# First group's key differences, queries and values loaded at other stages, last seeds stored after them, first maxima's rows put behind the first seeds

## The chip, the cores and the metric

The kernel runs on one core of a Trainium2 chip. The metric is the device time of one execution in microseconds; the time given is the median of several runs.

## The reference

Two independent halves are computed from float32 inputs and put side by side in the output, 2048 rows of 2 x 448.

```python
def _A_ref(u, log_A_real, A_imag, C_real, C_imag, log_dt, D_skip):     # D = 448, N = 256
    dt = jnp.exp(log_dt)
    A = -jnp.exp(log_A_real) + 1j * A_imag
    C = (C_real + 1j * C_imag) * dt[:, None]
    P = jnp.exp((A * dt[:, None])[:, :, None] * pos[None, None, :])
    K = 2.0 * jnp.einsum("dn,dnl->dl", C, P).real
    # y = causal convolution of u with K along the 2048 rows, by FFTs of length 4096
    return y + u * D_skip[None, None, :]

def _B_ref(x, wqkv, wo):                                               # 16 heads of 28
    q, k, v = (x @ wqkv) split into heads
    p = _softmax(einsum("bhqd,bhkd->bhqk", q, k) * Dh ** -0.5, axis=-1)
    return einsum("bhqk,bhkd->bhqd", p, v) merged @ wo
```

## The kernel before

The program has an opening, in which the projections of the attention and the "seeds" of the convolution kernel are computed and written to device memory, and a long second part that works through 16 units of attention, with the convolution's work put into slots between them.

**The opening.** It is a loop over 41 stages (`n_stage`). Each stage issues some of the 48 projection jobs (`work`): 4 chunks of 512 rows, in each 8 jobs for keys and queries (4 groups of heads, keys first: `qk_proj`) and 4 for values (`v_proj`; in the last chunk ahead of the keys). The jobs are spread evenly over the first 37 stages (`PW`). A job's matmuls go out in one call of `project`, its emptying from PSUM (`evac`) in the next: ScalarE writes a rounded high part into a tile `hl`, VectorE the remainder, and SyncE stores both to `k_d` or `q_d`. There are two `hl` tiles, so that a job's `evac` waits until the store of the job two before has landed. For the first two chunks `evac` also stores the key differences (`kd_d`).

Beside the projections run the seeds, in 8 parts (`seeds(o)`), four stages apart (`SP`); the 13 steps of a part go to successive stages (`slots`). The last two steps are its stores: `put_g` (tile `sg`, 11 stages after the part's start) and `put_e` (12 after). The tile that `put_e` stores is one of three tiles named `qhat`, the same three that hold the queries of a unit (`load_q`).

`ahead` says at which stage the first group's operands are loaded back: key differences (`load_kd`, 16 transfers, two a stage from stage `A0`), the first unit's queries (`load_q(0)`, two of its four transfers at stage `A1` and two at the next), keys of the heads 0 to 2 (`load_k(0, j)`, four transfers each, at the stages `KW`). The keys take the place of the projections' weights (`k0_t`), one head's place after another. In a stage, the seeds' steps and then `ahead` come behind the projections. At the last projection stage follow the fourth keys, the second unit's queries and the four tiles of values.

In this part no order is written by hand for the engines (`KEPT["p"]` is empty); a planner orders the instructions with the program's order as priority. All transfers are issued by SyncE.

After the loop come the row maxima of the first unit: 16 tiles, each with four matmuls (`max_mm`; the first reads the key differences, the other three the keys). The first matmul goes through ScalarE (`rl`), and VectorE reduces. `max_join` and `max_end` turn the maxima into two rows `mh`, and `max_put` stores those into two spare rows of the first unit's queries, so that the scores' matmul subtracts the maximum.

**The second part** keeps the program's order on every engine (`nc.kept = KEPT["a"]`). It begins with the loads of three parts of seeds (`load_sd`, tile `sdb`), the maxima of three tiles of the second unit (`LEAD`), the first use of the seeds, and the loads `u_load(0)` and `u_load(1)` (four transfers each, tile `ua`). Then come, for each of 256 steps, the scores (`s_mm`, tile `pss`), the exponentials, the product with the values (`po`), the maxima of the unit ahead, and a slot of the convolution.

All instructions are recorded under one helper line (L75), so that rows of the profile are told apart by their tiles.

Of the kernel before, what the change touches and what calls it, by code (L numbers as in the profile page):

```python
# [25 lines left out]
NQ = L // CQ  # L26
# [14 lines left out]
PS = 1  # L41
SGB, XB, XL = 2, 5, 4
K0, KP, KD, UP = 0, 3.5, 4, 3
A0, A1, KW = 26, 34, (33, 35, 36)

N1 = 32
N2 = 64
# [5 lines left out]
NO = 8  # L53
# [37 lines left out]
def body(ctx, tc, a, out):  # L91
# [53 lines left out]
    def load_k(g, j, p):  # L145
        if j == 0:
            t = k0_t if g == 0 else p.tile([128, HG, L], F32R, name="khat")
            kt_g[g] = [t[:, i] for i in range(HG)]
        for r in range(4):
            nc.sync.dma_start(kt_g[g][j][32 * r:32 * r + 32, :].bitcast(F32), k_d[g][r % 2, 32 * j:32 * j + 32, :])  # L150
# [3 lines left out]
    def load_v(g, c):  # L154
        v_g[g, c] = t = v_p.tile([128, NK // NQ, HG, 32], F32, name="v", bufs=5)
        nc.sync.dma_start(t.rearrange("p t h e -> p t (h e)"), v_d[c][:, g])
# [8 lines left out]
    def load_q(u, rows=range(4)):  # L165
        g, c = divmod(u, NQ)
        if 0 in rows:
            q_u[u] = q_p.tile([128, HG, CQ], F32R, name="qhat", bufs=3)
        t = q_u[u]
        for r in rows:  # L170
            nc.sync.dma_start(t[32 * r:32 * r + 32].bitcast(F32), q_d[g][c][r // 2].rearrange("(j p) q -> p j q", j=HG))
# [26 lines left out]
    def max_end(u, ps):  # L198
        nc.tensor.transpose(ps[:16, :128], m_u[u, 1], ident)
        mh = q_p.tile([16, 2, 128], F32R, name="mh")  # L200
        nc.vector.tensor_scalar(mh[:, 0, :], ps[:16, :128], -1.0, None, op0=ALU.mult)
        nc.vector.scalar_tensor_tensor(mh[:, 1, :], ps[:16, :128], -1.0, mh[:, 0, :].bitcast(F32),
                                       op0=ALU.mult, op1=ALU.subtract)
        mh_u[u] = mh

    def max_put(u):
        for i in range(2):
            nc.sync.dma_start(q_u[u][DH + i:DH + i + 1, :, :].rearrange("p h (t q) -> p (h t) q", t=4).bitcast(F32),
                                mh_u[u][:, i, :].bitcast(F32))


    with ExitStack() as st:
# [47 lines left out]
        t = a["A_log_dt"]  # L260
# [52 lines left out]
        def seeds(o):  # L313
# [87 lines left out]
            def factors(i, k, p_, n_):  # L401
                zz, mg = q["zz"], q["mg"]
                mul(vec, zz[:, i:i + 3, :, 0, :], vk(mg, k), vk(q["r"], k))
                mul(vec, zz[:, i:i + 3, :, p_, :], vk(mg, k), vk(q["sn"], k))
                for k in range(i, i + 3):
                    act.activation(zz[:, k, :, n_, :], zz[:, k, :, p_, :], AF.Copy, scale=-1.0)

            def cmul(e, dst, s0, n, wr, wi, conj):

                if e is nc.vector:  # L410
                    x_ = ps_x.tile([128, CQ], F32, name="px")[:, :BO * 16 * n].rearrange("p (b h e) -> p b h e", h=16, e=n)
                else:
                    x_ = s_p.tile([128, BO, 16, 4], F32, name="x_e")[:, :, :, :n]
                br, bi = (w_[:, :, :, None].to_broadcast([128, BO, 16, n]) for w_ in (wr, wi))
                for c in range(2):
                    mul(e, dst[c], s0[c], br)
                    mul(e, x_, s0[1 - c], bi)
                    e.tensor_tensor(dst[c], dst[c], x_, ALU.add if (c == 0) == conj else ALU.subtract)
# [3 lines left out]
            e3 = lambda: cmul(vec if o % 8 < E3 else pol, e8(3, 4), e8(1, 2), 1, q["e8"][:, :, 0, :, 2], q["e8"][:, :, 1, :, 2], False)  # L422
            e5 = lambda: cmul(pol, e8(5, 8), e8(1, 4), 3, q["e8"][:, :, 0, :, 4], q["e8"][:, :, 1, :, 4], False)
            put_e = lambda: nc.sync.dma_start(sd_d[o][:, :, :F_G].rearrange("b p f -> p b f"), q["se"])
            put_g = lambda: nc.sync.dma_start(sd_d[o][:, :, F_G:].rearrange("b p f -> p b f"), q["sg"])

            def load():
                if o not in nats:
# [2 lines left out]
            dts = lambda *r: [lambda i=i: times_dt(i) for i in r]  # L431
            fa, fb = lambda: factors(0, 3, 2, 1), lambda: factors(3, 8, 1, 2)
            return [[load], [exp_a] + dts(1, 2, 3), dts(0), [turn], [phases], [reduce], [sines], [sizes, g_base],
                    [places, fa, e_base], [e3, g_first], [fb, e5, g_copies], [put_g], [put_e]]

        xh, xl = {}, {}

# [58 lines left out]
        for c in range(NQ):  # L496
# [4 lines left out]
            if c + 1 < NQ:  # L501
                jobs[1] = (lambda c, f: lambda: (load_x(c + 1), f())[1])(c, jobs[1])
            work += jobs
        stages = [seeds(o) for o in range(NO)]
        n_stage = SP * (NO - 1) + len(stages[0])
        slots = [[] for _ in range(n_stage)]
        for o in range(NO):
# [5 lines left out]
        ahead = collections.defaultdict(list)  # L513
        for i in range(2 * HG):
            ahead[A0 + i].append(lambda i=i: load_kd(0, i // 2, range(2 * (i % 2), 2 * (i % 2) + 2)))
        for i in range(2):
            ahead[A1 + i].append(lambda i=i: load_q(0, range(2 * i, 2 * i + 2)))

        for j, t in enumerate(KW):
            ahead[t].append(lambda j=j: load_k(0, j, k0_p))  # L520

        def project():

            e = work.pop(0)() if work else None
            while pend:
                pend.pop(0)()
            if e:
                pend.append(e)

        for t in range(n_stage):  # L530
            while work and n_work - len(work) < n_work * (t + 1) / PW:
                project()
            for f in slots[t] + ahead.get(t, []):
                f()
            if t + 1 == PW:
                project()
                wst.close()
                load_k(0, HG - 1, k0_p)
                load_q(1)
                for c in range(NQ):  # L540
                    load_v(0, c)
        xst.close()
        more = [lambda: ps_t.tile([128, CQ], F32, name="pt")] * 2 + [w_tile] * 3
        for i in range(16):
# [2 lines left out]
        nc.scalar.activation(half_pi[:1], half_pi[:1], AF.Exp)  # L547
        max_join(0)
        max_end(0, ps_t.tile([128, CQ], F32, name="pt"))
        max_put(0)  # L550
        sst.close()


# [322 lines left out]
    def u_load(i):  # L876
        if i < 32:
            u_jobs[i][0]()
# [10 lines left out]

    u_load(0)  # L890
    u_load(1)
    u_due = collections.deque((3 + UP * i + (UP / 2) * c + (4 if i > 15 else 0), i, c) for i in range(32) for c in range(2))
    k_due = collections.deque(range(NB))
    m_due = collections.deque()
# [229 lines left out]
```

## Time and profile before

| | |
|---|---|
| median of 3 runs | 1322.6 us (1322.46 to 1323.23) |
| profiled execution | 1324.82 us |
| its span | 1323.0 us |
| mean granted TensorE clock | 0.973 |
| TensorE busy | 1235.2 us, 93% |
| VectorE, ScalarE, GpSimd busy | 75%, 72%, 63% |
| moved by DMA | 205.36 MB, 155 GB/s over the span |

The page and the trace are of one execution. PE is TensorE, PEld its weight loads, DVE VectorE, ACT ScalarE, POOL GpSimd, SPq the queue of SyncE, where an entry is the issue of a transfer and not the transfer itself. Times are microseconds from the start of the span. `khat` are keys (and, earlier, the projections' weights), `qhat` queries or a part's first seeds, `kdif` key differences, `sg` a part's other seeds, `mh` the maxima's rows, `rl` and `mx` the maxima's intermediate tiles.

### The profile page before, as it was taken

How to read it: one execution, taken by the hardware profiler on the slowest of the kernel's cores; microseconds unless marked ns; L12 is line 12 of the kernel's file. 1: busy time of each engine (PE TensorE's matmuls, PEld its weight loads, DVE VectorE, ACT ScalarE, POOL GpSimd, SP SyncE). 2: the span in 40 equal slices, each digit the busy share in tenths (PEclk: the TensorE clock that was granted, in tenths of full speed). 3: DMA queues.
4: the chain of work that ended last, by engine and by line, in shares of the span. 5: the costliest groups of instructions: out<-in, count | busy, mean ns of one | idle time of the engine just before them, and what ended most of it. 6: DMA issues, size and time to landing. Idle time of an engine off the chain costs nothing.

```text
span 1323.0 us, 33194 instructions
## 1 busy us (share of the span) xinstructions
PE 1235.2 (93%) x12625; PEld 705.6 (53%) x12625; DVE 989.7 (75%) x2138; ACT 953.3 (72%) x2068; POOL 839.9 (63%) x704
## 2 busy tenths in 40 slices
PE   6878886899999999999999999999998999898997
PEld 5657763455555555555555555555555545444433
DVE  5897786877778777778778988889887857757311
ACT  5876762488888888888888888888886656655553
POOL 3686682398887788887689999899992212211211
PEclk9979888899999999999999999999999999999999
DMA  6677669836765546478534134642325543824485
GB/s 204 204 263 257 218 210 286 230 69 139 183 146 133 128 137 172 130 182 215 165 99 93 55 85 94 149 96 56 97 56 146 189 154 132 276 91 165 148 221 137
DMA packets 200088, 205.36 MB, mean 155 GB/s; under 512 B 95992, under 2 KB 158520, under 8 KB 197880
## 3 DMA queue, kind: packets, MB, share of 16 engines
q1 hardware_dynamic: 199928, 203.23, 54.8%
q8 instruction: 100, 1.64, 0.5%
q14 instruction: 60, 0.49, 0.1%
HBM read 120.73 MB, written 82.18 MB: 153 GB/s over the span
## 4 chain that ended last, share of the span: by engine, by line
PE 69%; DVE 15%; POOL 5%; ACT 4%; issue 3%; DMA 2%; SPq 0%; ACTq 0%; POOLq 0%; DVEq 0%
PE pm L75 39%; PE po L75 15%; PE pss L75 15%; DVE mx L75 3%; DVE tri L75 2%; DVE p L75 2%; DVE pr L75 2%; DVE rl L75 1%; POOL e L75 1%; POOL qhat L75 1%; DVE qhat L75 1%; ACT tri L75 1%; DVE sg L75 1%; DVE px L75 1%; ACT p L75 1%
## 5 line engine op out<-in xcount | busy, mean ns | idle before, releaser
L75 ACT ACTIVATE p<-pss 128x512 f32<-128x512 f32 x1024 | 561.4, 610 | 120.8 <-PE pss L75 118.2
L75 PE MATMUL pss<-qhat,khat 128*128 128x512 f32 x1024 | 402.8, 399 | 2.3 <-ACT p L75 2.3
L75 DVE TENSOR_REDUCE mx<-pm 128x1 f32<-128x512 f32 x500 | 321.5, 684 | 101.8 <-PE pm L75 100.2
L75 PE MATMUL pm<-khat,qhat 128*128 128x512 f32 x749 | 327.1, 440 | 14.4 <-DVE mx L75 6.9
L75 POOL TENSOR_TENSOR e<-e,sdb 128x256 f32<-128x256 f32 x168 | 202.2, 1203 | 118.0 <-ACT e L75 108.8
L75 PE MATMUL po<-p,v 128*32 128x512 f32 x2048 | 270.1, 596 | 0.0
L75 POOL TENSOR_TENSOR e<-e,eu 128x256 f32<-128x256 f32 x168 | 248.4, 1479 | 13.2
L75 PEld LDWEIGHTS pm<-khat,qhat 128*128 128x128 f32 x749 | 141.6, 189 | 210.6 <-ACT p L75 43.6
L75 DVE CUSTOM_DVE_ANT_0 rl<-pm,rl 128x512 f32<-128x512 f32 x249 | 171.5, 689 | 59.9 <-ACT rl L75 56.0
L75 PEld LDWEIGHTS pss<-qhat,khat 128*128 128x128 f32 x1024 | 190.8, 189 | 47.8 <-issue 11.8
L75 POOL TENSOR_TENSOR eu<-e,sdb 128x256 f32<-128x256 f32 x168 | 202.3, 1204 | 0.0
L75 POOL TENSOR_TENSOR p<-pr,pr 64x448 f32<-64x448 f32 x32 | 40.9, 1279 | 197.5 <-DVE pr L75 186.5
L75 ACT ACTIVATE rl<-pm 128x512 f32<-128x512 f32 x249 | 150.9, 606 | 20.8 <-PE pm L75 20.7
L75 DVE TENSOR_TENSOR g<-g,zg 128x128 f32<-128x128 f32 x392 | 162.3, 414 | 3.4
L75 PE MATMUL pm<-xh,khat 112*128 112x512 f32 x256 | 92.9, 447 | 21.9 <-DVE hl L75 9.5
L75 PE MATMUL pm<-kdif,qhat 128*128 128x512 f32 x249 | 101.4, 407 | 2.4 <-DVE mx L75 1.3
L75 DVE TENSOR_TENSOR zg<-g,zg 128x128 f32<-128x128 f32 x224 | 88.0, 393 | 5.1
L75 PEld LDWEIGHTS pm<-e,g 128*32 128x32 f32 x3584 | 57.2, 109 | 43.7 <-issue 17.0
L75 PE MATMUL pm<-e,g 128*32 128x64 f32 x3584 | 73.1, 222 | 1.9 <-POOL e L75 1.9
L75 PEld LDWEIGHTS pm<-xh,khat 112*128 112x128 f32 x256 | 54.0, 216 | 37.8 <-DVE hl L75 10.9
L75 ACT ACTIVATE y<-pm 128x448 f32<-128x448 f32 x48 | 26.3, 549 | 66.1 <-issue 33.0
L75 PEld LDWEIGHTS po<-p,v 128*32 128x32 f32 x2048 | 55.8, 110 | 22.3 <-issue 17.9
(135 smaller groups left out, 1504.6 us busy)
## 6 DMA issues: line engine op xcount, KB each, us to landing
sdb<-sd SPq DMA_DIRECT2D x56, 336.0 KB
khat<-k SPq DMA_DIRECT2D x64, 256.0 KB
qhat<-q SPq DMA_DIRECT2D x64, 256.0 KB
sd<-sg SPq DMA_DIRECT2D x8, 1456.0 KB
k<-hl SPq DMA_DIRECT2D x16, 512.0 KB
q<-hl SPq DMA_DIRECT2D x16, 512.0 KB
mw<-in_mw SPq DMA_DIRECT2D x16, 512.0 KB
sd<-qhat SPq DMA_DIRECT2D x8, 896.0 KB
```

The source lines that it names most:

```text
L75: i = f(*args, **kw)
```

## The change

The key differences are loaded from stage 16 on instead of 26. The first unit's queries are loaded at the stages 33 and 34 instead of 34 and 35. Three of the four value tiles are loaded at the stages 14, 23 and 31; the fourth stays after the fourth keys. In each stage, `ahead` now comes before the projections and the seeds' steps instead of behind them. The stores of the last two parts of the seeds leave their stages: they follow the loop, those of part 6 before the second unit's queries and those of part 7 behind them. `max_put(0)` moves from the end of the opening into the second part, behind the first seed loads, the three lead tiles and the two `u` loads.

```diff
-A0, A1, KW = 26, 34, (33, 35, 36)
+A0, A1, KW, V0 = 16, 33, (33, 35, 36), (14, 23, 31)
...
-                    [places, fa, e_base], [e3, g_first], [fb, e5, g_copies], [put_g], [put_e]]
+                    [places, fa, e_base], [e3, g_first], [fb, e5, g_copies], [put_g], [put_e]], [put_g, put_e]
...
         stages = [seeds(o) for o in range(NO)]
+        put_last = [f for o in range(NO - 2, NO) for f in stages[o][1]]
+        stages = [t if o < NO - 2 else t[:-2] + [[], []] for o, (t, _) in enumerate(stages)]
...
+        for c, t in enumerate(V0):
+            ahead[t].append(lambda c=c: load_v(0, c))
         for j, t in enumerate(KW):
             ahead[t].append(lambda j=j: load_k(0, j, k0_p))
...
         for t in range(n_stage):
+            for f in ahead.get(t, []):
+                f()
             while work and n_work - len(work) < n_work * (t + 1) / PW:
                 project()
-            for f in slots[t] + ahead.get(t, []):
+            for f in slots[t]:
                 f()
             if t + 1 == PW:
                 project()
                 wst.close()
                 load_k(0, HG - 1, k0_p)
-                load_q(1)
-                for c in range(NQ):
-                    load_v(0, c)
+                load_v(0, NQ - 1)
+        for f in put_last[:2]:
+            f()
+        load_q(1)
+        for f in put_last[2:]:
+            f()
...
         max_end(0, ps_t.tile([128, CQ], F32, name="pt"))
-        max_put(0)
         sst.close()
...
     u_load(0)
     u_load(1)
+    max_put(0)
```

## The prediction

> **What bounds the kernel now.** I read the page first: after an opening of some 250 us TensorE is busy nearly all the time, so whatever moves the end of the opening moves the end of the kernel by as much.
>
> ```profile
> span 1323.0 us, 33194 instructions
> ...
> PE 1235.2 (93%) x12625; PEld 705.6 (53%) x12625; DVE 989.7 (75%) x2138; ACT 953.3 (72%) x2068; POOL 839.9 (63%) x704
> ```
>
> Every edit lies in the opening. So I read the chain of waits next, from 190 us to the first scores. Its pieces are start, duration, what.
>
> ```profile
> 37.77 3.51 DMA k<-hl
> ...
> 203.56 11.49 DMA qhat<-q
> ...
> 255.44 0.43 PE pss L75
> ```
>
> The chain stands for 11.49 us in one load: the queries of the first unit. TensorE's timeline says the same from its side, and those of ScalarE and VectorE show what stands at the same place (start, duration, engine, operation, and in brackets the idle time before it and what ended it).
>
> ```profile
> 203.31 0.40 PE L75 MATMUL pm<-xl,khat 112*128 112x512 f32 x1
> 215.19 0.76 PE L75 MATMUL pt<-kdif,qhat 128*128 128x512 f32 x1 [11.48 <-DMA qhat<-q]
> ```
>
> ```profile
> 198.77 0.57 ACT L75 ACTIVATE hl<-pm 128x512 fp32r<-128x512 f32 x1
> 205.38 0.69 ACT L75 ACTIVATE hl<-pm,kones 128x512 fp32r<-128x512 f32 x1 [6.04 <-DMA k<-hl]
> ...
> 210.51 0.63 ACT L75 ACTIVATE hl<-pm 128x512 fp32r<-128x512 f32 x1
> ```
>
> ```profile
> 206.10 0.75 DVE L75 SCALAR_TENSOR_TENSOR hl<-pm,kones,hl 128x512 fp32r<-128x512 f32 x1 [3.49 <-ACT hl L75]
> ...
> 211.17 0.69 DVE L75 TENSOR_TENSOR hl<-pm,hl 128x512 fp32r<-128x512 f32 x1 [1.05 <-ACT hl L75]
> 216.62 0.69 DVE L75 CUSTOM_DVE_ANT_0 rl<-pt,rl 128x512 f32<-128x512 f32 x1 [4.76 <-ACT rl L75]
> ...
> 248.54 0.28 DVE L75 SCALAR_TENSOR_TENSOR mh<-pt,mh 16x128 fp32r<-16x128 f32 x1
> ```
>
> The projections end on TensorE at 203.71 (203.31 + 0.40), the first maximum begins at 215.19. But VectorE is done with the last projection only at 211.86 (211.17 + 0.69) and starts on the maxima at 216.62. From there to the finished maxima at 248.82 (248.54 + 0.28) it works through the first unit's tiles. So of TensorE's 11.48 us only VectorE's 4.76 can come back by an earlier load alone.
>
> Why the load is late stands in SyncE's queue, the only one that issues transfers, in program order:
>
> ```profile
> 180.25 0.47 SPq L75 DMA_DIRECT2D sd<-sg  x1
> ...
> 184.42 1.29 SPq L75 DMA_DIRECT2D sd<-qhat  x1
> ...
> 194.93 0.38 SPq L75 DMA_DIRECT2D q<-hl  x1
> ...
> 196.79 1.76 SPq L75 DMA_DIRECT2D khat<-k  x4
> ...
> 202.04 0.50 SPq L75 DMA_DIRECT2D sd<-sg  x1
> 202.59 1.78 SPq L75 DMA_DIRECT2D qhat<-q  x2
> ...
> 219.76 6.01 SPq L75 DMA_DIRECT2D khat<-k  x4
> ...
> 248.53 1.26 SPq L75 DMA_DIRECT2D qhat<-mh  x2
> 249.85 1.52 SPq L75 DMA_DIRECT2D sdb<-sd  x3
> 251.41 4.62 SPq L75 DMA_DIRECT2D ua<-in_A_u  x8
> ```
>
> The sizes of one transfer, from the page, and the traffic by stretch (length, engines' busy time, granted clock, share of the DMA engines, GB/s):
>
> ```profile
> sdb<-sd SPq DMA_DIRECT2D x56, 336.0 KB
> khat<-k SPq DMA_DIRECT2D x64, 256.0 KB
> qhat<-q SPq DMA_DIRECT2D x64, 256.0 KB
> sd<-sg SPq DMA_DIRECT2D x8, 1456.0 KB
> k<-hl SPq DMA_DIRECT2D x16, 512.0 KB
> ...
> sd<-qhat SPq DMA_DIRECT2D x8, 896.0 KB
> ...
> kdif<-kd SPq DMA_DIRECT2D x64, 64.0 KB
> v<-v SPq DMA_DIRECT2D x16, 256.0 KB
> ...
> ua<-in_A_u SPq DMA_DIRECT2D x64, 56.0 KB
> ```
>
> ```profile
> 80.00:110.00 30.00, 23.09 (x84) 18.62 (x84) 26.26 (x44) 23.75 (x49) 22.68 (x29) 0.80 0.52 181
> 180.00:192.00 12.00, 12.00 (x45) 9.48 (x43) 11.83 (x20) 6.05 (x8) 11.45 (x7) 0.82 1.03 358
> ...
> 196.00:248.00 52.00, 34.24 (x88) 18.77 (x86) 38.68 (x85) 15.11 (x31) 9.53 (x15) 0.82 1.03 286
> 228.00:236.00 8.00, 7.14 (x19) 3.09 (x18) 8.00 (x19) 2.61 (x5) 0.00 (x0) 1.00 1.05 244
> ```
>
> From 196 to 248 us the transfers run at their limit: four key loads take SyncE 6.01 us to issue at 219.76, 1.76 at 196.79. Order in the queue is order of landing there. I take stores at 358 GB/s (180 to 192 us is mostly stores) and loads at 244 (228 to 236 us is keys and queries): 512 KB stored 1.46 us, 1456 KB 4.16, 896 KB 2.56; a key load of 4 x 256 KB 4.30, half the queries 2.15. Before the first byte comes 2.05 us: the 3.51 of the unhurried store at 37.77 less 1.46. Tested on before, from 194.93: store of query rows 198.4, two key differences 199.0, keys 203.3, store 204.7, half the queries 206.9, store 208.3, seeds 212.5, other half 214.6. The trace has 205.38 for the fourth (ScalarE's wait) and 215.05 for the last (203.56 + 11.49): the walk is 0.4 to 0.7 us early, and I add 0.5.
>
> **The change, part by part.**
>
> *Key differences and values sooner.* Sixteen loads of 64 KB and three of 256 KB go to stages 14 to 31; nothing is added. The differences fall at about 80 to 125 us, where the DMA engines are 0.52 busy at 80 to 110; by 244 GB/s the sixteen take 4.3 us of 30. I take nothing for it. Its cover gone, it delays a projection's store, whose buffer ScalarE waits for: there is one such wait of 2.2 us at 60 to 90 us, so I bound it by 2.2 either way.
>
> ```profile
> ACT hl L75 <- DMA k<-hl: 2.2, 1, 2.2
> ```
>
> *First queries and keys sooner, last seeds later.* Half the queries and the first keys now stand behind the seeds of 184.42 and ahead of two projection stores; the other half behind the store of 194.93; the seeds of 202.04 behind the last keys. The walk, from 180.25: seeds 186.5, store 187.9, seeds 190.5, half the queries 192.6, keys 196.9, stores 198.4 and 199.9, other half 202.0, store 203.5, second keys 207.8, store 209.2. With 0.5 added the queries are there at 202.5, ahead of TensorE's 203.71, and leave the chain.
>
> *What is late next* is the emptying of the projections: VectorE at 211.86, ScalarE at 211.14 (210.51 + 0.63). Its own waits are for buffers, freed when earlier stores land. Against before, the store that ScalarE awaited at 205.38 lands 1.2 us sooner; the one freed for 198.77 comes at 200.4, 1.6 later; the one freed for 210.51 at 209.7, still in time. Bounds: VectorE's idle 3.49 us at 206.10 may go altogether, or the 1.6 and 0.9 (209.2 against 208.3) may both be lost, 2.5. Between them I take nothing, as the sooner and the later one meet in the same row. Gain: 4.76 us.
>
> The Trainium skill, "DMA: Bandwidth & Descriptors", section "Queues, rings and completion order", says that each DMA engine takes one issuing engine's descriptors in ring order. That speaks against putting 1.5 MB of loads ahead of the stores that ScalarE waits for. ScalarE's 6.04 us for a store agree. By this rule alone, with nothing landing sooner, the sum would be 4.76 - 2.5 = 2.3.
>
> *Second queries.* Their tile is one from which seeds are stored, so SyncE now waits at this load for a store just issued, and holds the last seeds and all below. The walk goes on: third keys 213.5, two stores 216.4, last keys 220.7, values 221.8, seeds 226.0 and 228.5, wait 2.05, queries 234.9. First use is after the maxima, 4.76 sooner than 248.82: 244.1. Nine us to spare: cost nothing.
>
> *Seeds and u ahead of the maxima's rows.* Those two small transfers now stand behind the last seeds (239.0, 241.6), three seed loads (1008 KB, 245.8) and eight of u (448 KB, 247.7): landed at about 248.7 with 0.5 added and 0.5 for themselves. SyncE issues the eleven while the maxima still run, before they cost 6.1 us after. The scores need the rows at 255.44 - 4.76 = 250.7, since the three lead tiles of the second unit stand ahead on TensorE. Two us to spare: cost nothing, gain nothing.
>
> Sum: 4.76 us. The profiled execution took 1324.82 us (span 1323.0), the median of the runs 1322.6. 1324.82 - 4.8 = 1320.0; the same off the median gives 1317.8. From 255 us on each engine keeps its order, so the shift reaches the end. The bound for a difference that can be told is 0.2%, 2.65 us.
>
> **The rivals.**
>
> *More comes back.* With the store of 205.38 sooner and no other later, VectorE's 3.49 us go too: 4.76 + 3.49 = 8.25, time 1314.3. For it: the walk has that store 1.2 sooner. Against: two others later.
>
> *The stores are late.* Both delays are lost (2.5) and a third wait of like size, 0.7, comes at the store landing at 198.9 for ScalarE's step just before 198.77: 4.76 - 3.2 = 1.6, time 1321.0, no difference to be told. For it: the order of the queue, and the rule above from "DMA: Bandwidth & Descriptors" of the Trainium skill. Against: the row of 6.04 gets shorter. That the change does not do what it says belongs here: no order is kept by hand in this phase, and a planner that left the loads where they were would give 1322.6. Before's queue follows the program text, so I hold that unlikely.
>
> *The maxima's rows become the wait*, and the kernel slower. From 199.9 to these rows SyncE now moves 13,072 KB, 13.39 MB. At the 286 GB/s of 196 to 248 us that is 46.8, with the 2.05 at the second queries 248.8. The gain is gone when the rows land at 255.44: 13.39 MB in 53.5 us, 250 GB/s. At the 225 GB/s of the stretch below it is 59.5 us, the rows come at 261.5, 6.0 late: 1328.6. For it: loads alone ran at 244. Against: the mix is before's, which made 286.
>
> ```profile
> 195.00:203.00 8.00, 8.00 (x22) 6.32 (x23) 5.20 (x12) 4.31 (x12) 5.45 (x11) 0.60 0.87 225
> ```
>
> **How the numbers follow.** Forecast 0.60, more comes back 0.15, stores late 0.15, maxima's rows 0.10. Faster by over 0.2%: 0.60 + 0.15 = 0.75; within 0.2%: 0.15; slower: 0.10. The likeliest gives 1317.8. The range goes down to 1314.3, the second case, and up to 1323.0, which holds the third and leaves the fourth out.
>
> **What would show it.** In the chain after, no load of the first queries; the first kdif matmul right after the projections or at VectorE's pace, its first reduction at 211 to 213; the stored maxima near 244; the first scores near 250.7, ended by a lead tile and not by a load. Late stores would show as longer idle times of ScalarE before hl than 6.04 us in all. If the first scores wait for the maxima's rows, the last part is wrong. If the opening shifts before 180 us, the first part is.

## The result: slower by 0.4%, because the opening was ordered anew

| | before | after |
|---|---|---|
| median | 1323.22 us (1322.46 to 1324.79) | 1328.43 us (1326.58 to 1330.24) |
| ratio, 95% interval | | 1.0039 [1.0026, 1.0053] |
| profiled execution | 1324.82 us | 1330.24 us |
| TensorE's last projection ends | 203.71 us | 216.12 us |
| first maximum starts on TensorE | 215.19 us | 215.91 us |
| maxima's rows ready on VectorE | 248.82 us | 254.86 us |
| first scores start | 255.24 us | 260.90 us |

The forecast was 1317.8 us, the range ended at 1323.0, and slower had a chance of 0.10.

The page of after answers to the first lines shown of before. TensorE has 5.1 us more to show as busy and the span is 5.5 us longer.

```profile
span 1328.5 us, 33194 instructions
...
PE 1240.3 (93%) x12625; PEld 708.9 (53%) x12625; DVE 986.7 (74%) x2138; ACT 955.4 (72%) x2070; POOL 836.3 (63%) x704
```

The chain of waits of after, at the place where before's had 11.49 us for the first queries (start, duration, what):

```profile
200.07 8.95 DMA k<-hl
...
209.10 0.70 ACT hl L75
...
209.82 0.76 DVE hl L75
...
210.63 5.49 PE pm L75 x12
216.12 0.83 PE pt L75 x2
```

No load of queries stands in it. A projection's store does: ScalarE can't empty the next projection before it has landed, and the last projection's matmuls follow. TensorE's timeline says the same: the first `kdif` matmul comes right behind the last projection, with no idle time named, and the scores follow lead tiles, not a load.

```profile
215.49 0.63 PE L75 MATMUL pm<-xl,khat 112*128 112x512 f32 x1
215.91 0.63 PE L75 MATMUL pt<-kdif,qhat 128*128 128x512 f32 x1
...
260.56 0.51 PE L75 MATMUL pm<-kdif,qhat 128*128 128x512 f32 x1
260.90 0.39 PE L75 MATMUL pss<-qhat,khat 128*128 128x512 f32 x1
```

VectorE's last step on the maxima's rows ends at 254.86, 6.0 us later than in before:

```profile
254.58 0.28 DVE L75 SCALAR_TENSOR_TENSOR mh<-pt,mh 16x128 fp32r<-16x128 f32 x1
```

So the wait that the change was aimed at is gone, and the projections in front of it have slipped by 12.4 us (216.12 less 203.71). The net at the scores is 5.66 us: 260.90 less 255.24, where before has its first scores:

```profile
255.24 0.63 PE L75 MATMUL pss<-qhat,khat 128*128 128x512 f32 x1
```

From there to the end both kernels take the same: 1067.8 us before (1323.0 less 255.24), 1067.6 after.

The slip begins long before 180 us. The planner has put all five queues of the opening in another order, from about 72 us on. The inputs of the seeds' parts 6, 7 and 8 show it best. (Parts are counted from 1 here, so these are `seeds(5)` to `seeds(7)`; the stores that the change moves are those of `seeds(6)` and `seeds(7)`.) First SyncE's queue: the issue of the first of the four loads of a part, three rows of before, then three of after.

```profile
96.14 0.82 SPq L75 DMA_DIRECT2D nat<-in_A_log_A_real  x1
...
122.72 0.87 SPq L75 DMA_DIRECT2D nat<-in_A_log_A_real  x1
...
140.07 0.83 SPq L75 DMA_DIRECT2D nat<-in_A_log_A_real  x1
```

```profile
114.67 0.87 SPq L75 DMA_DIRECT2D nat<-in_A_log_A_real  x1
...
143.97 0.82 SPq L75 DMA_DIRECT2D nat<-in_A_log_A_real  x1
...
162.13 1.39 SPq L75 DMA_DIRECT2D nat<-in_A_log_A_real  x1
```

Then ScalarE's first step on each of these parts, the exponential, again before and after:

```profile
105.11 0.42 ACT L75 ACTIVATE nat<-nat 56x256 f32<-56x256 f32 x1
...
134.24 0.42 ACT L75 ACTIVATE nat<-nat 56x256 f32<-56x256 f32 x1
...
148.12 0.42 ACT L75 ACTIVATE nat<-nat 56x256 f32<-56x256 f32 x1
```

```profile
121.60 0.42 ACT L75 ACTIVATE nat<-nat 56x256 f32<-56x256 f32 x1
...
151.18 0.42 ACT L75 ACTIVATE nat<-nat 56x256 f32<-56x256 f32 x1
...
171.02 0.41 ACT L75 ACTIVATE nat<-nat 56x256 f32<-56x256 f32 x1
```

The inputs are issued 18.5, 21.3 and 22.1 us later, the steps come 16.5, 16.9 and 22.9 us later. No idle time before these steps is put down to a load, since the planner has put the steps themselves behind other work. A reader who looks only for waits on transfers doesn't see the cost there; comparing the places of the same instruction in the two traces shows it.

It shows in TensorE's waits too: the seeds share ScalarE and VectorE with the emptying of the projections. From 57 us to the end of the last projection, these are two of its waits before (total, times, longest), then after; `vst` are the values that ScalarE empties:

```profile
PE pm L75 <- DVE hl L75: 11.8, 4, 5.4
...
PE pm L75 <- ACT vst L75: 2.5, 1, 2.5
```

```profile
PE pm L75 <- DVE hl L75: 19.2, 6, 6.9
PE pm L75 <- ACT vst L75: 9.6, 4, 4.4
```

With those for the key differences (`kb`) and the transposed inputs (`xl`), 5.4 and 2.8 us before and 0.7 and 5.2 after, TensorE's waits in this stretch grow from 22.5 to 34.7 us. That is 12.2 of the 12.4 us by which the projections slipped.

### The profile page after: what moved, and what is told of

Its sections match the earlier page's. It is cut to its first block, busy times and chain, and to the rows that moved or that the text cites. A ratio compares the mean times of both kernels' runs of the same rounds, so it can differ in the third digit from the quotient of the medians.

```text
span 1328.5 us, 33194 instructions
## 1 busy us (share of the span) xinstructions
PE 1240.3 (93%) x12625; PEld 708.9 (53%) x12625; DVE 986.7 (74%) x2138; ACT 955.4 (72%) x2070; POOL 836.3 (63%) x704
## 4 chain that ended last, share of the span: by engine, by line
PE 68%; DVE 14%; POOL 6%; issue 4%; ACT 4%; DMA 3%; SPq 1%; POOLq 0%; ACTq 0%; DVEq 0%
PE pm L75 38%; PE pss L75 15%; PE po L75 15%; DVE mx L75 3%; POOL e L75 2%; DVE p L75 2%; DVE tri L75 2%; DVE pr L75 2%; POOL qhat L75 1%; DVE rl L75 1%; POOL tri L75 1%; DMA k<-hl 1%; ACT p L75 1%; DVE sg L75 1%; POOL eu L75 1%
```

## The experiments

Theory: the planner's new order of the opening costs more than the change brings, and with before's order the change does what was predicted. Rivals: the moved loads cost by their own traffic; or the tail of the change (last seeds, rows) is what loses.

To tell order from traffic, several kernels hold the order of an engine's opening as it was in the kernel before. The instructions of the opening are recorded as the program issues them, and each is tied to its predecessor in the wanted order; the ties lie inside one engine's own queue. In the traces the held engines run the same sequence of operations, tiles and shapes as in before (in e3, as in after). In kernels with this code the helper line has another number, L83 to L87.

```python
for e, order in PINNED.items():
    seq = [OPEN_REC[e][k] for k in order]
    for x, y in zip(seq, seq[1:]):
        ...                                # y behind x on e, order only
```

Each run stands against runs of the kernel before on the same chip. Rows of one letter share a chip; between letters the ratios are to be compared, not the medians.

| run | edit in short | median us | ratio, 95% interval |
|---|---|---|---|
| e1 | before + last seeds late + rows behind u | 1323.41 | 0.9997 [0.9985, 1.0008] |
| f3 | before + last seeds late | 1319.39 | 0.9970 [0.9961, 0.9979] |
| e4 | before + early loads, planner free | 1327.24 | 1.0025 [1.0016, 1.0034] |
| f1 | before + early loads, all queues held | 1323.03 | 0.9995 [0.9985, 1.0004] |
| f2 | after, all queues held | 1321.33 | 0.9989 [0.9979, 0.9999] |
| f4 | early loads + last seeds late, all held | 1320.33 | 0.9971 [0.9960, 0.9982] |
| e2 | after, all held but SyncE | 1329.21 | 1.0040 [1.0028, 1.0053] |
| g2 | e2 with the seeds' inputs early | 1320.73 | 0.9987 [0.9975, 0.9999] |
| g1 | before, all held, the seeds' inputs late | 1330.94 | 1.0065 [1.0048, 1.0081] |
| e3 | before, computing engines in after's order | 1340.64 | 1.0127 [1.0113, 1.0141] |
| h1 | after, SyncE alone held | 1336.40 | 1.0081 [1.0066, 1.0095] |
| i1 | h1, ScalarE held too | 1325.82 | 1.0015 [1.0005, 1.0025] |
| i2 | h1, TensorE held too | 1341.44 | 1.0134 [1.0121, 1.0147] |
| g3 | after without the early loads, planner free | 1324.77 | 1.0018 [1.0004, 1.0032] |

**The tail alone (e1), and without the rows' move (f3).** Neither edit changes the order of a computing engine, so the planner isn't in the way here.

```diff
-                load_q(1)                      # in the loop, at the last projection stage
-                for c in range(NQ):
-                    load_v(0, c)
+        for f in put_last[:2]:                 # behind the loop: stores of seeds(6)
+            f()
+        load_q(1)
+        for c in range(NQ):
+            load_v(0, c)
+        for f in put_last[2:]:                 # stores of seeds(7)
+            f()
...
-        max_put(0)                             # e1 only
...
     u_load(1)
+    max_put(0)                                 # e1 only
```

> The kernel before with only the two edits at the end of the opening: the last two parts' seeds are stored behind the loop (part 6 ahead of the second unit's queries, part 7 behind them), and the first maxima's rows stand behind the first seed loads. Every load keeps its old stage. In the built program the order of the four computing engines is that of before, only 14 places of SyncE's queue differ. Order theory (the early loads made the planner put the opening's computing in another, slower order; the end of the opening gains): the first queries no longer stand behind 1456 KB of seeds, 2 to 5 us faster than before, 1318 to 1321. Traffic theory (the early loads themselves delay the projections' stores): the same, since no early load is in it. End theory (stores last and rows behind are what costs): slower than before, 1326 or more.

> The kernel before with the last two parts of the seeds stored behind the loop, and the maxima's rows stored at their old place, right after the maxima. The test of the tail had the maxima ready 4.2 us sooner, but their rows' store was issued 7.3 us behind them, after the loads of seeds and u. If that place ate the gain: the first scores start 4 us sooner, near 251.3, and the time is 1319 to 1320.5. If the scores were held by something else (the second queries, the seeds, the lead tiles): no change, 1323 to 1324.

e1 fell between its ranges, 1323.41, neither the gain of the first case nor the loss of the last. In it the rows were ready at 244.59 us, 4.23 before the kernel before, and the first scores started at 254.58, only 0.66 sooner. SyncE's queue and TensorE's timeline of e1 show where the rest went:

```profile
242.82 8.96 SPq L75 DMA_DIRECT2D ua<-in_A_u  x8
251.88 1.28 SPq L75 DMA_DIRECT2D qhat<-mh  x2
```

```profile
254.58 0.77 PE L75 MATMUL pss<-qhat,khat 128*128 128x512 f32 x1 [3.37 <-DMA qhat<-mh]
```

The two small stores were issued 7.3 us after the rows were ready, because the eight loads of u were 8.96 us in the issuing. In f3 the stores are issued at once, and the scores start behind lead tiles, 4.4 us before those of the kernel before:

```profile
244.12 1.26 SPq L75 DMA_DIRECT2D qhat<-mh  x2
```

```profile
211.28 0.76 PE L75 MATMUL pt<-kdif,qhat 128*128 128x512 f32 x1 [8.22 <-DMA khat<-k]
...
250.82 0.56 PE L75 MATMUL pss<-qhat,khat 128*128 128x512 f32 x1
```

So the late seeds alone brought the first maximum from 215.19 to 211.28, though no query was loaded at another stage: those seeds had stood ahead of the queries in the queue. And the place behind u cost all of it: 0.9997 of before with it (e1), 0.9970 without (f3).

**The early loads, with the planner free (e4) and with all queues held (f1).** The same edit twice; in f1 only the 19 moved loads stand at other places of SyncE's queue.

```diff
-A0, A1, KW = 26, 34, (33, 35, 36)
+A0, A1, KW, V0 = 16, 34, (33, 35, 36), (14, 23, 31)
...
+        for c, t in enumerate(V0):
+            ahead[t].append(lambda c=c: load_v(0, c))
```

> The kernel before with only the early loads: key differences from stage 16 and three tiles of values at 14, 23 and 31; the planner is free, and puts 70 places on TensorE and 158 on VectorE otherwise. Order theory: the opening loses about what it lost in after, without the gain at the end: 1328 to 1336. Traffic theory: 1326 to 1332. End theory: 1322 to 1325.

> The kernel before with the key differences from stage 16 on and three value tiles at the stages 14, 23, 31, and nothing else of the change. The order of all four computing engines in the opening is held as in the kernel before, and in SyncE's queue every transfer but these 19 keeps its place, so the seeds' inputs are issued as early as before. If it was the planner's new order of all queues that cost the 3.3 us of the early loads: no change, 1323 to 1324.5, the last projection ends near 203.7. If the loads' own traffic delays the projections' stores: 1326 to 1328, the last projection ends near 207 to 209.

Free, they cost 0.25%; held, nothing that can be told. e4 alone didn't tell the theories apart: 1327.24 lies in the range for traffic and just below the one for order. f1 does: the traffic is not the cost, and the ties by themselves cost nothing that can be told either. In e4 the exponential of part 6 is late as in after:

```profile
121.27 0.42 ACT L75 ACTIVATE nat<-nat 56x256 f32<-56x256 f32 x1
```

In f1 the wait for the first queries stands as in before, so there was nothing to gain by these loads alone:

```profile
213.44 0.80 PE L87 MATMUL pt<-kdif,qhat 128*128 128x512 f32 x1 [10.96 <-DMA qhat<-q]
```

**The kernel after with all queues held (f2), and the best of both (f4).** f2 is the kernel that the prediction walked through: the engines in before's order, SyncE in before's order but for the transfers that the change names. f4 leaves out the sooner first queries and keys and the rows' move.

```diff
-A0, A1, KW, V0 = 16, 33, (33, 35, 36), (14, 23, 31)
+A0, A1, KW, V0 = 16, 34, (33, 35, 36), (14, 23, 31)      # f4; and ahead behind the seeds' steps, max_put(0) at its old place
...
+    for e, order in PINNED.items(): ...                   # f2, f4: all four engines and SyncE
```

> The kernel after, with the computing engines' opening order held as before and SyncE's queue held as before too but for the transfers that the change names. This is the kernel that the prediction walked through. If the planner's order was the fault of the prediction: the last projection ends near 204 to 206, the finished maxima stand near 244 to 247, and the time is 1319 to 1323, the lower end where the rows' store, now behind the first seeds and u, is no wait, the upper end where it lands at 253 to 254 as in the test of the tail. If the early loads and the first keys ahead of the stores cost by themselves: the last projection ends at 208 or later, 1325 to 1329.

> The kernel before with the early key differences and values, the last seeds stored late, the rows' store at its old place and the first queries at their old stage; the order of all engines held as before but for the transfers named. If the planner's order and the rows' place are the two costs of the change: 1318 to 1320.5, faster than both kernels. If the early traffic costs by itself: 1322 to 1325.

The same program text as after, in another order, takes 0.9989 of before's time, where after takes 1.0039, and is no longer slower than before. Its TensorE has no wait for queries, and its scores none for the rows:

```profile
208.16 0.39 PE L87 MATMUL pt<-kdif,qhat 128*128 128x512 f32 x1
...
252.25 0.50 PE L87 MATMUL pm<-kdif,qhat 128*128 128x512 f32 x1
252.59 0.40 PE L87 MATMUL pss<-qhat,khat 128*128 128x512 f32 x1
```

The time lies in the range that was expected, but the last projection ends at 208.33, not at 204 to 206. What is late in f2 is the emptying of the projections. ScalarE's and VectorE's timelines:

```profile
201.63 0.69 ACT L87 ACTIVATE hl<-pm,kones 128x512 fp32r<-128x512 f32 x1 [3.15 <-DMA k<-hl]
...
206.85 0.69 ACT L87 ACTIVATE hl<-pm,kones 128x512 fp32r<-128x512 f32 x1 [3.85 <-DMA k<-hl]
213.27 0.60 ACT L87 ACTIVATE hl<-pm 128x512 fp32r<-128x512 f32 x1 [1.06 <-DMA q<-hl]
```

```profile
213.90 0.69 DVE L87 TENSOR_TENSOR hl<-pm,hl 128x512 fp32r<-128x512 f32 x1 [2.28 <-ACT hl L87]
...
245.90 0.28 DVE L87 SCALAR_TENSOR_TENSOR mh<-pt,mh 16x128 fp32r<-16x128 f32 x1
```

One wait of 6.04 us for a store has become three of 8.06 together, and VectorE ends the last projection at 214.59 where it was 211.86. The rows are ready at 246.18, 2.64 sooner than before; in f4, without the queries and keys ahead of those stores, they are ready at 244.48.

**The seeds' inputs in SyncE's queue: e2, g2, g1.** e2 holds the four computing engines and leaves SyncE to the planner. g2 is e2's queue, transfer by transfer, with twelve loads moved back to where before has them. g1 is the kernel before, with the same twelve loads put late and nothing else moved.

```diff
 # SyncE's order, g1 (parts 7 and 8 likewise)
-q_2 store, nat 6 (4 loads), k_3 store, kd_3 store, q_3 store, v_1 store
+q_2 store, k_3 store, kd_3 store, q_3 store, v_1 store, nat 6 (4 loads)
```

> The kernel after, with the order of the opening's instructions on TensorE, VectorE, ScalarE and GpSimd pinned to that of before; SyncE's queue is left to the planner and has all the early loads. Order theory: the 12.7 us by which the last projection was late go, the gain at the end stays: 1317 to 1319. Traffic theory: 1326 to 1330, as after. End theory: 1326 to 1330.

> The test of the old order (1329.2) with its queue kept transfer by transfer, except that the twelve input loads of the seeds' parts 6, 7 and 8 are issued where the kernel before has them, behind the query stores. If the late inputs are the cost: the wait for them goes, chunk 2 of x is transposed near 113 us again instead of 117.7, and the time is 1321 to 1324. If other places of that queue cost it too (the first queries' load ahead of value stores, the stores of seeds behind key differences): 1326 to 1329.

> The kernel before with every queue kept, except that SyncE issues the four input loads of the seeds' parts 6, 7 and 8 later, each behind the same store as in the test of the old order (behind the first value store of chunk 2, the second key store of chunk 3, the first value store of chunk 3). No load is moved sooner and no store is moved. If the late inputs are what the planner's queue costs: the wait of ScalarE for them near 100 us is back (7.0 us there), the last projection ends 4 to 8 us later, 1327 to 1331. If it is the stores and the first queries in that queue: no change, 1323 to 1324.5.

If the order of the computing engines were the whole cost, e2 should have taken 1317 to 1319 us. It took 1329.21: with all four held, the planner's queue alone loses as much as after does. g1 and g2 say what in it. With the engines' old order the late inputs are to be seen as waits. e2, then g1, each with the parts 6 and 8; then part 6 of f2, whose inputs are early:

```profile
112.78 0.42 ACT L86 ACTIVATE nat<-nat 56x256 f32<-56x256 f32 x1 [7.00 <-DMA nat<-in_A_log_A_real]
...
158.72 0.42 ACT L86 ACTIVATE nat<-nat 56x256 f32<-56x256 f32 x1 [5.33 <-DMA nat<-in_A_log_A_real]
```

```profile
111.81 0.42 ACT L87 ACTIVATE nat<-nat 56x256 f32<-56x256 f32 x1 [6.71 <-DMA nat<-in_A_log_A_real]
...
155.68 0.42 ACT L87 ACTIVATE nat<-nat 56x256 f32<-56x256 f32 x1 [2.95 <-DMA nat<-in_A_log_A_real]
```

```profile
105.18 0.42 ACT L87 ACTIVATE nat<-nat 56x256 f32<-56x256 f32 x1
```

Twelve small loads, of 56 x 256 numbers each, issued 11 to 13 us later, make 0.65% on the kernel before (g1), and putting them back takes 0.53% off e2 (1.0040 to 0.9987). The 9.66 us of g1's two waits stand against 8.6 us of time (0.0065 of 1322.6). This holds for the engines in before's order.

**The computing engines' order: e3, h1, i1, i2, g3.** e3 puts the four computing engines of the kernel before into after's order. h1 is after with SyncE held as in f2 and the four engines left to the planner; i1 and i2 hold ScalarE or TensorE as well. g3 takes the early loads out of after.

```diff
 PINNED = {
+    "sync": ...,          # h1, i1, i2: as in f2
+    "scalar": ...,        # i1: as in before
+    "tensor": ...,        # i2: as in before
 }
...
-A0, A1, KW, V0 = 16, 33, (33, 35, 36), (14, 23, 31)
+A0, A1, KW, V0 = 26, 33, (33, 35, 36), ()               # g3; no PINNED
```

> The kernel before, with the order of the opening's instructions on the four computing engines pinned to that of the kernel after; all transfers at their old stages. Order theory: the last projection some 10 to 13 us late and the end of the opening no faster: 1329 to 1336. Traffic theory: 1322 to 1325, as before. End theory: 1322 to 1325.

> The kernel after with SyncE's queue alone held as in the test that kept all queues (1321.3); the four computing engines are left to the planner, which orders them otherwise than before again. If late inputs in the queue are the whole cost and the engines' other order only follows from them: 1320 to 1323.5, the last projection ends near 208. If the planner's order of the computing engines costs by itself, as its order on the kernel before did (1340.6): 1325 to 1330, the last projection ends at 212 or later.

> The kernel after with SyncE's queue held as in the test that kept all queues, and of the computing engines only ScalarE's order held as before; TensorE, VectorE and GpSimd are the planner's. If the planner's late seeds' steps (first exponential of part 7 at 148.7 us with the queue alone held, 134.2 before) are what its order of the engines costs: 1320 to 1324, part 7 begins near 136. If the places of the projections on TensorE are: 1328 or more.

> The kernel after with SyncE's queue held as in the test that kept all queues, and of the computing engines only TensorE's order held as before; ScalarE, VectorE and GpSimd are the planner's. If the planner's places of the projections on TensorE are what its order of the engines costs: 1320 to 1324. If it is the seeds' late steps on ScalarE and VectorE: 1328 or more, part 7 begins behind 140.

> The kernel after with the key differences back at stage 26 and the values behind the fourth keys; the first queries, the order within a stage, the last seeds and the rows' place as in the kernel after; the planner free. Its order differs from before's too. If only the early loads draw the planner into the bad order: the last projection ends near 204 to 208 and the time is 1320 to 1324. If any move of loads in the opening does it: 1326 to 1330.

The order of the engines costs by itself. In e3 it is after's own, no load is moved to another stage, and SyncE, left to the planner, issues the inputs of the three parts at 90.4, 121.9 and 132.9 us, no later than before. It is still 1.27% slower, more than was expected: the exponential of part 6 comes at 123.52 and the last projection ends at 215.35, nearly as late as in after (216.12). Behind that its first maximum still waits 7.08 us for the queries.

h1 is the other way round, f2's order of SyncE with the planner's engines: 1.0081 against 0.9989, again more than expected. Its order of the engines is not after's but a third one: of ScalarE's 277 instructions in the opening, 123 stand at another place than in before and 119 at another than in after. And although the order of the transfers is f2's, SyncE comes to the three parts' inputs later, at 101.7, 131.7 and 165.0 us instead of 97.7, 124.4 and 141.7; the exponentials show no wait for them. Here are those of the parts 7 and 8, which f2 has at 135.90 and 149.77: h1, then i1, then i2.

```profile
148.74 0.42 ACT L83 ACTIVATE nat<-nat 56x256 f32<-56x256 f32 x1
173.62 0.42 ACT L83 ACTIVATE nat<-nat 56x256 f32<-56x256 f32 x1
```

```profile
138.07 0.42 ACT L84 ACTIVATE nat<-nat 56x256 f32<-56x256 f32 x1
154.13 0.44 ACT L84 ACTIVATE nat<-nat 56x256 f32<-56x256 f32 x1
```

```profile
140.99 0.42 ACT L84 ACTIVATE nat<-nat 56x256 f32<-56x256 f32 x1
168.45 0.42 ACT L84 ACTIVATE nat<-nat 56x256 f32<-56x256 f32 x1
```

With ScalarE's order held too, i1 comes back from 1.0081 to 1.0015, and the seeds' steps with it. That doesn't show ScalarE's order to be the one that counts: with it held, the planner put most of VectorE and GpSimd back as well (66 of 341 and 8 of 154 instructions at another place than in before, against 160 and 50 in h1). With TensorE's order held instead, i2 is slower than h1, 1.0134, although its seeds' steps come 7.8 and 5.2 us sooner than h1's. So late steps of the seeds alone don't account for the time either. Which engine's order loses it, or which two orders don't fit each other, is open. i1's 1325.82 lies 1.8 us above what was expected.

g3 came out between its two cases, 1324.77: without the early loads the planner's order seems to lose less (1.0018 against 1.0039, with intervals that overlap), but it still differs from before's, and the exponential of part 8 is late there (163.52). It doesn't settle which edit draws the planner off.

What is shown for after as built, then: its order is the cause (f2 against after, the same text), and two parts of such an order cost by themselves, late inputs in SyncE's queue (g1, g2) and the order of the computing engines (e3, h1). In after both come together, and since its steps are so late no wait for the inputs is left. The two don't add up: the last projection ends at 213.63 with the queue alone the planner's (e2), at 215.35 with after's order of the engines alone (e3), and at 216.12 in after. How the 0.50% between after and f2 (1.0039 less 0.9989, 6.6 us of 1322.6) divides between the two was not measured, and no run opened the planner's own reckoning to show why it chose so.

## Why the prediction was wrong, step by step

- **The step that failed: that the built order would stay as it was.** The prediction held that "Before's queue follows the program text" and that the change moves only the transfers it names, so that nothing shifts ahead of them. Not even before's queue follows the text throughout: its SyncE issues the inputs of part 6 ahead of stores that come first in the text (the first line of g1's diff). In after the planner moved all five queues, and the last projection ended at 216.12 instead of 203.71. The prediction named a planner that doesn't follow under *the stores are late*, but priced it at no change (1322.6), as one that leaves loads where they were. Between f2 and after it measured 0.50%. The prediction's last sentence named the sign by which to see it, a shift before 180 us; the chance for it was missing.
- ***Key differences and values sooner: nothing.*** Right as traffic (f1, 0.9995), wrong as an edit (e4, 1.0025). The bound of 2.2 us came from a wait for a store; the cost came from the planner's answer to 19 loads at another place.
- ***The queries leave the chain.*** Right in after and f2. But f3 shows that the late seeds alone do nearly all of it at the maxima: 4.41 us (248.82 to 244.41) of the 4.76.
- ***What is late next: 4.76.*** Mis-sized, as f2 shows. Its emptying ended 2.73 us later than before's, and the rows gained 2.64: about the lower bound of the gain (2.5 lost), and not the middle that the prediction chose. The walk had the stores landed too early: three that it put at 198.9, 204.0 and 209.7 (with the 0.5 added) release ScalarE's steps only at 201.63, 206.85 and 213.27. Why the first of them landed late is open. In time f2 gained 0.11%, 1.5 us of 1322.6, which is the rival *the stores are late* (1.6, 1321.0), and its sign came too, 8.06 us of waits in place of 6.04. The Trainium skill, "DMA: Bandwidth & Descriptors", section "Queues, rings and completion order", says that each DMA engine takes one issuing engine's descriptors in ring order. f2's trace agrees, with 2.64 at the rows where the prediction had 2.3 by that rule alone; no run tests the rule by itself.
- ***Second queries, seeds and u ahead of the rows: nothing.*** Right in f2, where the rows were ready at 246.18 and no wait for their store is shown at 252.59. But the rows of f2 came late enough to hide it: in e1, with the rows 1.6 us sooner, the same place cost the scores 3.37 us of waiting. The two us to spare of the prediction rested on its walk, which had the rows landed at 248.7. f2 issues their stores only from 248.43 to 249.71, e1 from 251.88 on.
- ***The maxima's rows become the wait.*** Not what made after slower: its scores at 260.90 show no such wait. It is what kept e1 from gaining. That the price of this rival, 1328.6, lies beside the measured 1328.43 is chance.
- ***From 255 us on the shift reaches the end.*** Right: 1067.8 and 1067.6 us from the first scores to the end, 1067.3 in f3. The largest deviation among the runs is e1's 1069.3.

The version that beats both kernels is f3, one edit of the change: 1319.39 us, 0.9970 [0.9961, 0.9979] of the kernel before. f4, with the early loads and the old order, is the same within its interval.

## What to carry to other kernels

Where a planner orders the engines, an edit is a request for a new plan: before costing what is moved, compare the built order of every engine, and where it has changed, hold the old order to see what the edit itself does. A late start of side work need not show as a wait of its own; look up the same instruction in both traces and compare its time, and see whether the busiest engine waits longer for what shares an engine with it. Holding one engine alone makes a new plan of the others, and so is no test of that engine (i1, i2). A store that the next stage needs is better ahead of bulk loads in the queue than behind them, even if the bulk loads seem hidden (f3 against e1).

## What was not expected of the hardware

Eight loads of u take SyncE 8.96 us to issue in e1 (from 242.82), against 4.96 us in f3 (at 247.00) and 4.62 in before (at 251.41). e1's trace says what SyncE waits for between these issues: the landing of the last seeds' two stores, 1.5 and 2.4 us, and of the three seed loads, 2.0. So the place of a small store behind such a group is not a matter of counting issues: the same group held it for 9 us in one kernel and would have for 5 in another. And twelve loads of 56 KB, 0.7 MB of the 205 MB moved, were worth 8.6 us by their place alone (g1).
